# Clip to SBUF, exponential in place: attention with hashed buckets and a gated feed-forward

## The chip, the core and the metric

The kernel runs on one core of one Trainium2 chip. A core has TensorE (PE; its weight loads are listed apart as PEld), VectorE (DVE), ScalarE (ACT), GpSimd (POOL) and SyncE (SP, which here only issues DMAs), with a shared memory of 128 partitions (SBUF), and PSUM, into which TensorE writes. Each engine works through its own list of instructions in order and waits on semaphores for the others. The metric is the device time of one execution in microseconds. "Before" is the kernel without the change, "after" the kernel with it.

## The reference

Attention over buckets, for 4 batches, 8 heads, 768 positions and 64 columns a head, followed by a gated feed-forward:

```python
q_bits = (np.einsum('bhsd,dk->bhsk', q, proj) > 0).astype(np.int64)   # k_bits likewise
q_bucket = np.sum(q_bits * powers, axis=-1)                           # 6 bits
mask = q_bucket[:, :, :, None] == k_bucket[:, :, None, :]
scores = scale * np.matmul(q, k.transpose(0, 1, 3, 2))
scores = np.where(mask, scores, -1000000000.0)
scores = scores - np.max(scores, axis=-1, keepdims=True)
attn = np.exp(scores)
attn = attn / (np.sum(attn, axis=-1, keepdims=True) + 1e-09)
return np.matmul(attn, v).astype(np.float32)
```

A query whose bucket holds no key has the same score, -1e9, everywhere. Its softmax is flat, and its result is the mean of V. The heads' results, side by side (512 columns), then go through

```python
h = np.maximum(x @ w_in, 0.0)
u, v = (h[..., :d_ff // 2], h[..., d_ff // 2:])
v_n = (v - mu) / np.sqrt(var + 1e-06)
v_s = np.einsum('ts,bsd->btd', w_spatial, v_n) + b_spatial[None, :, None]
return ((u * v_s) @ w_out).astype(np.float32)
```

## The kernel before

**Numbers.** TensorE multiplies in f16. Each f32 operand is split into a high and a low f16 part. q and k are scaled by 32 for this. The hash bits of q and k are further rows of the same operands, so that the score matmuls themselves add a penalty, a multiple of 2^29 in the scaled scores, for each bit that differs. A score below -2^28 is thus one of an unmatched pair. The factor ISQ (1/8192) takes scaled scores back.

**Tiles.** There are 32 heads (n), each with six tiles (i) of 128 queries by 768 keys: global step g = 6n + i. Heads go in pairs p = n // 2, whose q, k and v are loaded together. Heads 1 to 7 (`KEYS`) have their keys on the partitions and go a way of their own (`row_max`, `scores_k`, `weighted_k`); they need the rows' maximum before the scores, but no transposition. The other 25 heads have queries on the partitions, 150 tiles in all. Such a tile passes these lines:

- L291, L292 (PE): four matmuls make the 128 x 768 scores in `sp`, a PSUM tile of two banks. There are two buffers of it (`PSB`).
- L293 (DVE): one pass over PSUM multiplies by -ISQ and takes the minimum along the row into `nb` (one column of a [128, 6] tile a head). The pass has to write its elements somewhere, and writes them as bf16 into the room of `ex` (`jk`), where nobody reads them.
- L294 (ACT): ex = exp(ISQ * scores + nb), from PSUM into SBUF, f32.
- L297 (ACT): the high f16 part of `ex`; L298: the low part, ex minus high, on DVE or, for one or two of six tiles, on POOL (`PL_POOL1`, `PL_POOL`).
- L300 (SP): a DMA transposes both halves, 128 x 1536 f16, into `pt`.
- L313 to L315 (PE): 18 matmuls with `pt` as weights add up the row of the result, and, through a column of ones beside V, the row's sum. They come five steps behind the scores (`LAG`).

**End of a head.** `normalize` (L317) divides by the sum. A row without a match has nb > ISQ * 2^28. For it the quotient is multiplied by zero (L329, DVE), and the mean of V times a flag (L323, L324, POOL) is added (L332, POOL). L337 and L338 split the sum `x` into f16 parts, and after the pair's second head L343 transposes them for the feed-forward. The mean of V comes from `mean_v`, once a pair: three additions on POOL (L224, L226, L227), a matmul with a matrix of ones (L229, f32, which TensorE runs as two), and a scaled copy (L231, ACT).

**Feed-forward.** The 28 units of batch b (`mlp_units`: v_unit, u_unit, s_unit, o_unit) are strewn among the tiles of batch b + 1, so many a step; the last batch's come at the end, with no attention beside them. The weights' conversion (`weights_gen`, L137 to L144) is strewn over steps 4 to 73 (`W_PTS`).

**What sets the order.** The program is traced step by step. `at(g, k)` sets a priority before each part, and a scheduler then fixes every engine's order at build time, by priority and by a planned timeline. Tiles of a tag share so many buffers (`bufs`): `ex` has EB = 3, `pp` PB = 4, `pt` PTB = 6; a new tile waits until the old one's last reader is done. SP issues nearly all DMAs: loads, the copies that build the operands (`build`, L192), transposes and results. ACT issues the hash rows' copies from head 8 on (L200, `BQ_S`).

## Time and profile before

| | |
|---|---|
| time, median of 3 runs | 726.72 us (724.35 to 730.93) |
| time of the profiled execution | 729.71 us |
| span of its instructions | 727.9 us |
| mean granted TensorE clock | 0.957 |
| busy: PE, PEld | 622.9 us (86%), 393.2 us (54%) |
| busy: DVE, ACT, POOL | 520.4 us (71%), 434.2 us (60%), 326.6 us (45%) |
| DMA | 120.96 MB, 290013 packets |

The profile's span runs from the first to the last instruction; the device time of the same execution is 1.8 us longer. A row of a group names the line, the engine, the operation, the tile written and those read (`out<-in`), the shape, and the count; then the busy time in us and the mean duration in ns, then the engine's idle time just before these instructions and what ended it. `ex<-sp` reads: writes `ex`, reads `sp`. A wait is put down to the one that was released last. "Chain" is the chain of work that ended last, followed backwards from the last instruction.

### The profile page before, as it was taken

What the parts mean: (1) busy time and instruction counts of PE and PEld (TensorE: products, weight loads), DVE (VectorE), ACT (ScalarE), POOL (GpSimd) and SP (SyncE); (2) the same over time, 40 slices, a digit from 0 to 9 for tenths busy, and PEclk for the clock granted to TensorE, in tenths of its full rate; (3) what the DMA queues carried; (4) which work ended last, traced back from release to release, by engine and by line L of the source; (5) the groups of instructions that cost most, each with busy time, mean ns of one, the idle gap of its engine ahead of it and who ended that gap; (6) DMA issues with size and microseconds to landing.
All of it is one profiled execution on the core that took longest, in us unless ns stands there. A gap on an engine that the chain in (4) does not pass through costs nothing. (4 is left out here: it accounts for less than half of the span.)

```text
span 727.9 us, 14930 instructions
## 1 busy us (share of the span) xinstructions
PE 622.9 (86%) x5759; PEld 393.2 (54%) x5759; DVE 520.4 (71%) x945; ACT 434.2 (60%) x668; POOL 326.6 (45%) x324
## 2 busy tenths in 40 slices
PE   1569897997987876998898899898989888999997
PEld 0237676875554543555555555565555555654553
DVE  4677894537899999768689887778699685845100
ACT  1345674356888677656667666667677677634221
POOL 5122542134479755446316672446146462441603
PEclk9969997999999988999999999999999999999999
DMA  9674745315999999997999999999999899860011
GB/s 238 151 140 146 170 132 105 94 47 131 233 247 210 212 198 203 218 210 161 223 213 186 193 202 183 228 197 206 228 227 169 167 168 210 147 157 10 1 44 44
DMA packets 290013, 120.96 MB, mean 166 GB/s; under 512 B 270741, under 2 KB 273813, under 8 KB 289941
## 3 DMA queue, kind: packets, MB, share of 16 engines
q1 hardware_dynamic: 287636, 119.11, 77.9%
q10 hardware_dynamic: 2304, 0.89, 0.5%
q8 instruction: 45, 0.74, 0.4%
q14 instruction: 28, 0.22, 0.1%
HBM read 28.33 MB, written 6.29 MB: 48 GB/s over the span
## 5 line engine op out<-in xcount | busy, mean ns | idle before, releaser
L294 ACT ACTIVATE ex<-sp,nb 128x768 f32<-128x768 f32 x150 | 134.6, 900 | 95.3 <-DVE ex L293 91.2
L293 DVE TENSOR_SCALAR_CACHE_REDUCE ex<-sp 128x768 bf16<-128x768 f32 x150 | 141.8, 949 | 43.2 <-PE sp L292 42.4
L298 DVE TENSOR_TENSOR pp<-ex,pp 128x768 f16<-128x768 f32 x116 | 125.9, 1091 | 20.7 <-ACT pp L297 20.5
L313 PE MATMUL pv<-vp,pt 128*128 128x65 f16 x900 | 105.5, 196 | 34.0 <-DMA pt<-pp 33.5
L291 PE MATMUL sp<-ab 128*128 128x384 f16 x300 | 102.2, 341 | 32.8 <-ACT ex L294 22.0
L297 ACT CAST pp<-ex 128x768 f16<-128x768 f32 x150 | 123.8, 830 | 10.6 <-ACT ex L294 2.5
L313 PEld LDWEIGHTS <-pt 128*128 128x128 f16 x900 | 85.4, 100 | 59.3 <-DMA pt<-pp 48.6
L298 POOL TENSOR_TENSOR pp<-ex,pp 128x768 f16<-128x768 f32 x34 | 58.2, 1711 | 123.9 <-ACT pp L297 101.1
L416 PE MATMUL sps<-ws,vn 128*128 128x384 f16 x576 | 103.9, 333 | 3.0 <-DVE sg L179 2.2
L314 PE MATMUL pv<-vp,pt 128*128 128x64 f16 x900 | 105.6, 195 | 0.0
L315 PE MATMUL pv<-vp,pt 128*128 128x65 f16 x900 | 105.3, 197 | 0.0
L292 PE MATMUL sp<-ab 127*128 127x384 f16 x300 | 102.4, 341 | 0.0
L314 PEld LDWEIGHTS <-pt 128*128 128x128 f16 x900 | 85.8, 99 | 10.7 <-issue 2.0
L315 PEld LDWEIGHTS <-pt 128*128 128x128 f16 x900 | 85.7, 99 | 3.7 <-issue 0.6
L416 PEld LDWEIGHTS <-vn 128*128 128x128 f16 x576 | 56.0, 100 | 40.7 <-issue 7.5
L431 PE MATMUL ops<-wo,g 128*128 128x512 f16 x288 | 70.0, 387 | 2.9 <-POOL wo L144 1.0
L401 PE MATMUL ups<-xt,wi 128*128 128x384 f16 x384 | 68.8, 331 | 0.0
L360 PE MATMUL vps<-wi,xt 128*128 128x512 f16 x288 | 67.1, 379 | 1.3 <-DMA xt<-xs 1.3
L332 POOL TENSOR_TENSOR x<-x,xf 128x384 f32<-128x384 f32 x32 | 36.8, 1151 | 69.7 <-DVE x L331 62.8
L274 PEld LDWEIGHTS pv<-vf,ex 128*128 128x128 f32 x504 | 65.6, 200 | 3.9 <-issue 1.1
L274 PE MATMUL pv<-vf,ex 128*128 128x65 f32 x504 | 64.5, 279 | 0.0
L421 POOL TENSOR_TENSOR sy<-sy,u 128x384 f32<-128x384 f32 x32 | 37.9, 1183 | 40.3 <-DVE sy L420 36.8
(87 smaller groups left out, 1006.1 us busy)
## 6 DMA issues: line engine op xcount, KB each, us to landing
qk<-kq SPq DMA_DIRECT2D x16, 768.0 KB
ab<-hl SPq DMA_DIRECT2D x31, 384.0 KB
ab<-hl SPq DMA_DIRECT2D x34, 192.0 KB
out<-o SPq DMA_DIRECT2D x24, 256.0 KB
v<-v SPq DMA_DIRECT2D x13, 384.0 KB
raw<-w_in SPq DMA_DIRECT2D x16, 256.0 KB
pt<-pp SPq DMA_TRANSPOSE x150
raw<-w_sp SPq DMA_DIRECT2D x12, 192.0 KB
```

What stands on the lines that cost most here:

```text
L274: nc.tensor.matmul(acc[:, qi, :], lhsT=ex[:, qi * P:(qi + 1) * P], rhs=vf[p % 2][:, 2 * i + e, :], start=(i == 0 and qi == 0), stop=(i == ...
L291: nc.tensor.matmul(ps[:, c], lhsT=t[:, 0, qs], rhs=t[:, 1, cs], start=True, stop=False)
L292: nc.tensor.matmul(ps[:, c], lhsT=t[0:P - 1, 3, qs], rhs=t[0:P - 1, 2, cs], start=False, stop=True)
L293: nc.vector.tensor_scalar(jk, ps, -ISQ, None, op0=ALU.mult, op1=ALU.min, accum_out=nb)
L294: st["ex", n, i] = nc.scalar.activation(ex, ps, AF.Exp, bias=nb, scale=ISQ).ins
L297: nc.scalar.copy(pp[:, 0], ex)
L298: (nc.gpsimd if i in (PL_POOL if n >= 2 * NH else PL_POOL1) else nc.vector).tensor_tensor(out=pp[:, 1], in0=ex, in1=pp[:, 0], op=ALU.subtract)
L313: nc.tensor.matmul(acc, lhsT=pt[:, c, :], rhs=vh, start=(i == 0 and c == 0), stop=False)
L314: nc.tensor.matmul(acc[:, 0:D], lhsT=pt[:, c, :], rhs=vl, start=False, stop=False)
L315: nc.tensor.matmul(acc, lhsT=pt[:, NT + c, :], rhs=vh, start=False, stop=(i == NT - 1 and c == NT - 1))
L416: nc.tensor.matmul(ps[:, :HS], lhsT=vn[gv][:, c, d * P:(d + 1) * P], rhs=ws[gw][:, c, hs], start=(k == 0), stop=(k == 3 * NT - 1))
L431: nc.tensor.matmul(ps, lhsT=gt[h][gg][:, c, j * P:(j + 1) * P], rhs=wo[gw][:, c, :], start=(k == 0), stop=(k == 3 * NF - 1))
```

## The change

For the 25 heads with queries on the partitions:

- The pass over PSUM now writes max(score, -2^28) as f32 into `ex` and takes the row's maximum into `mx`; the bf16 room is gone. A new operation on DVE makes nb = -ISQ * mx for the tile's column. The exponential reads `ex` in SBUF and writes it in place, so that the PSUM tile's last reader is the pass on DVE.
- A row without a match has -2^28 everywhere, so the exponential gives 1 in every place, and the quotient is the mean of V by itself. `normalize` loses the flag, the product with the mean, the zeroing and the addition in these heads.
- `mean_v` is left out for pairs without a key-oriented head (pairs 4 to 15). Its two scratch tiles, and the one in `normalize`, move to the tags `g0`, `g1` and `u`, which the feed-forward uses too; the tags `pf` and `vc` are gone.
- `ex` has four buffers in place of three, `mx` four in place of two.

In the heads 1 to 7 `normalize` keeps the flag, the product and the addition, and loses only the zeroing (L329), as their quotients there come out as zero.

```diff
@@ -218,11 +218,13 @@
         nc.vector.scalar_tensor_tensor(out=t[:, :, 0:D], in0=v32, scalar=SQ, in1=t[:, :, D:2 * D], op0=ALU.mult, op1=ALU.subtract)
 
     def mean_v(p):
+        if not has_keys(p):
+            return
         v32 = st["v32", p] if has_queries(p) else vf[p % 2][:, :, 0:D]
 
-        a = wk.tile([P, NT, D], F32, tag="pf", name=f"va{p}")
+        a = wk.tile([P, NT, D], F32, tag="g0", name=f"va{p}")
         nc.gpsimd.tensor_add(a, v32[:, 0:NT], v32[:, NT:2 * NT])
-        c = wk.tile([P, 2, D], F32, tag="vc", name=f"vc{p}")
+        c = wk.tile([P, 2, D], F32, tag="g1", name=f"vc{p}")
         nc.gpsimd.tensor_add(c, a[:, 0:2], a[:, 2:4])
         nc.gpsimd.tensor_add(c, c, a[:, 4:6])
         mp = ps_m.tile([P, 512], F32, tag=MT, name=f"mp{p}")
@@ -234,7 +236,7 @@
     def row_max(n, i):
         t = ab[n % NAB]
         if i == 0:
-            st["mx", n] = wk.tile([P, NT], F32, tag="mx", bufs=2, name=f"mx{n}")
+            st["mx", n] = wk.tile([P, NT], F32, tag="mx", bufs=4, name=f"mx{n}")
         ps = ps_sc.tile([P, 2, 512], F32, tag="sc", name=f"mp{n}_{i}")[:, :, :HS]
         for c in range(2):
             nc.tensor.matmul(ps[:, c], lhsT=t[0:P - 1, 3, i * P:(i + 1) * P],
@@ -281,17 +283,18 @@
         t = ab[n % NAB]
         if i == 0:
             st["nb", n] = wk.tile([P, NT], F32, tag="nb", bufs=3, name=f"nb{n}")
-        nb = st["nb", n][:, i:i + 1]
+            st["mx", n] = wk.tile([P, NT], F32, tag="mx", bufs=4, name=f"mx{n}")
+        mx, nb = st["mx", n][:, i:i + 1], st["nb", n][:, i:i + 1]
         ex = wk.tile([P, 2, HS], F32, tag="ex", bufs=EB, name=f"ex{n}_{i}")
-        jk = ex.rearrange("p c k -> p (c k)").bitcast(BF16)[:, 0:S].rearrange("p (c k) -> p c k", c=2)
         qs = slice(i * P, (i + 1) * P)
         ps = ps_sc.tile([P, 2, 512], F32, tag="sc", name=f"sp{n}_{i}")[:, :, :HS]
         for c in range(2):
             cs = slice(c * HS, (c + 1) * HS)
             nc.tensor.matmul(ps[:, c], lhsT=t[:, 0, qs], rhs=t[:, 1, cs], start=True, stop=False)
             nc.tensor.matmul(ps[:, c], lhsT=t[0:P - 1, 3, qs], rhs=t[0:P - 1, 2, cs], start=False, stop=True)
-        nc.vector.tensor_scalar(jk, ps, -ISQ, None, op0=ALU.mult, op1=ALU.min, accum_out=nb)
-        st["ex", n, i] = nc.scalar.activation(ex, ps, AF.Exp, bias=nb, scale=ISQ).ins
+        nc.vector.tensor_scalar(ex, ps, -float(2 ** 28), None, op0=ALU.max, op1=ALU.max, accum_out=mx)
+        nc.vector.tensor_scalar(nb, mx, -ISQ, None, op0=ALU.mult)
+        st["ex", n, i] = nc.scalar.activation(ex, ex, AF.Exp, bias=nb, scale=ISQ).ins
         at(NT * n + i + G_H, 50)
         pp = wk.tile([P, 2, 2, HS], F16, tag="pp", bufs=PB, name=f"pp{n}_{i}")
         nc.scalar.copy(pp[:, 0], ex)
@@ -317,19 +320,21 @@
     def normalize(n):
         p, e = divmod(n, 2)
         pv = st.pop(("pv", n))
-        nb = st.pop(("nb", n))
-        fl = wk.tile([P, NT], F32, tag="fl", bufs=2, name=f"fl{n}")
-        f = wk.tile([P, NT, D], F32, tag="pf", name=f"xf{n}")
-        nc.gpsimd.tensor_scalar(fl, nb, ISQ * 2 ** 28, None, op0=ALU.is_gt)
-        nc.gpsimd.tensor_mul(f, st["fm", p][:, e:e + 1, :].to_broadcast([P, NT, D]),
-                             fl.unsqueeze(2).to_broadcast([P, NT, D]))
         rv = wk.tile([P, NT], F32, tag="rv", bufs=2, name=f"rv{n}")
         nc.vector.tensor_scalar(rv, pv[:, :, D], 1e-9, 1.0 / SX if n in KEYS else SQ / SX, op0=ALU.add, op1=ALU.mult)
         nc.vector.reciprocal(rv, rv)
-        nc.vector.scalar_tensor_tensor(out=rv, in0=nb, scalar=ISQ * 2 ** 28, in1=rv, op0=ALU.is_le, op1=ALU.mult)
         x = wk.tile([P, NT, D], F32, tag="x", bufs=2, name=f"x{n}")
-        nc.vector.tensor_mul(x, pv[:, :, 0:D], rv.unsqueeze(2).to_broadcast([P, NT, D]))
-        nc.gpsimd.tensor_add(x, x, f)
+        if n in KEYS:
+            nb = st.pop(("nb", n))
+            fl = wk.tile([P, NT], F32, tag="fl", bufs=2, name=f"fl{n}")
+            f = wk.tile([P, NT, D], F32, tag="u", name=f"xf{n}")
+            nc.gpsimd.tensor_scalar(fl, nb, ISQ * 2 ** 28, None, op0=ALU.is_gt)
+            nc.gpsimd.tensor_mul(f, st["fm", p][:, e:e + 1, :].to_broadcast([P, NT, D]),
+                                 fl.unsqueeze(2).to_broadcast([P, NT, D]))
+            nc.vector.tensor_mul(x, pv[:, :, 0:D], rv.unsqueeze(2).to_broadcast([P, NT, D]))
+            nc.gpsimd.tensor_add(x, x, f)
+        else:
+            nc.vector.tensor_mul(x, pv[:, :, 0:D], rv.unsqueeze(2).to_broadcast([P, NT, D]))
         if e == 0:
             st["xs", p] = wk.tile([P, 2, NT, P], F16, tag="xs", bufs=2, name=f"xs{p}")
         xs = st["xs", p]
@@ -462,7 +467,7 @@
 
     RB = 3
     PB = 4
-    EB = 3
+    EB = 4
     PTB = 6
     XTB = 6
     LAG = 5
```

## The prediction

> **What bounds the kernel now.** The stretches of the span come first, because a share over the whole span mixes stages with different limits. The columns are busy time (and count) of TensorE, its weight loads, VectorE, ScalarE and GpSimd, then the granted clock, the share of the DMA engines and GB/s.
>
> ```profile
> 200.00:300.00 100.00, 77.05 (x821) 47.27 (x820) 97.43 (x163) 76.68 (x133) 69.18 (x59) 0.93 1.03 214
> 300.00:400.00 100.00, 89.74 (x939) 55.41 (x936) 77.50 (x145) 65.91 (x98) 43.94 (x41) 0.98 0.97 200
> 400.00:500.00 100.00, 89.62 (x941) 56.30 (x939) 80.56 (x137) 67.78 (x94) 50.64 (x45) 0.95 1.01 199
> 500.00:600.00 100.00, 90.20 (x950) 54.45 (x948) 82.86 (x154) 70.64 (x104) 49.48 (x44) 0.98 1.04 195
> 600.00:650.00 50.00, 47.43 (x537) 30.58 (x538) 33.76 (x64) 30.93 (x44) 20.80 (x20) 1.00 0.82 169
> 650.00:728.00 78.00, 72.59 (x393) 38.10 (x391) 14.72 (x36) 19.70 (x40) 22.98 (x23) 1.00 0.11 36
> ```
>
> There are three limits. From 200 to 300 us VectorE is busy 97.43 of 100 us: the conversion of the weights runs there beside the attention. From 300 to 650 us no engine is full: TensorE has 90 of 100, VectorE 77 to 83, and the DMA engines show shares of 0.97 to 1.04, so they are close to full as well. From 650 us on TensorE does the last batch's feed-forward nearly without a gap (72.59 of 78), and nothing of the change is in it. Before 170 us there are head 0 and the seven key-oriented heads, which the change leaves as they are but for head 0 (six tiles); I put that at 0.
>
> Next, what TensorE waits for between 180 and 650 us (total, times, longest).
>
> ```profile
> PE pv L313 <- DMA pt<-pp: 28.4, 28, 3.4
> PE sp L291 <- ACT ex L294: 19.5, 15, 2.6
> PE mp L229 <- POOL vc L227: 3.2, 5, 1.2
> ```
>
> The largest wait is for the transposed probabilities, which DMA brings. The second is for the exponential: score matmuls need one of two PSUM buffers, and the exponential of two tiles earlier holds it. The third is for GpSimd's sum of V. The change takes away the last two; where these waits lie decides what that is worth.
>
> Groups from 200 to 300 us, and from 300 to 650 us (busy, mean ns | idle before, its releaser):
>
> ```profile
> L293 DVE TENSOR_SCALAR_CACHE_REDUCE ex<-sp 128x768 bf16<-128x768 f32 x28 | 26.3, 946 | 1.7 <-PE sp L292 1.5
> L291 PE MATMUL sp<-ab 128*128 128x384 f16 x56 | 19.3, 344 | 13.5 <-ACT ex L294 13.4
> L329 DVE SCALAR_TENSOR_TENSOR rv<-nb,rv 128x6 f32<-128x6 f32 x4 | 0.8, 192 | 0.0
> L376 DVE TENSOR_SCALAR ve<-mv 128x3 f32<-128x3 f32 x2 | 1.8, 885 | 0.0
> ```
>
> ```profile
> L293 DVE TENSOR_SCALAR_CACHE_REDUCE ex<-sp 128x768 bf16<-128x768 f32 x104 | 98.4, 949 | 32.6 <-PE sp L292 32.0
> L291 PE MATMUL sp<-ab 128*128 128x384 f16 x206 | 68.2, 331 | 6.1 <-ACT ex L294 6.1
> L229 PE MATMUL mp<-vc,ones 128*128 128x128 f32 x16 | 3.9, 331 | 2.4 <-POOL vc L227 2.4
> L329 DVE SCALAR_TENSOR_TENSOR rv<-nb,rv 128x6 f32<-128x6 f32 x19 | 5.8, 306 | 0.5
> L376 DVE TENSOR_SCALAR ve<-mv 128x3 f32<-128x3 f32 x4 | 1.4, 354 | 0.0
> ```
>
> 13.4 us of the wait for the exponential lie in the stretch where VectorE is full, and only 6.1 us after it. In the first stretch the exponential is late because VectorE's clip pass before it is late, so freeing PSUM sooner gives VectorE no time back. Only the 6.1 us count.
>
> **The VectorE part.** The clip pass (L293) still reads 768 PSUM floats per partition and now writes f32 instead of bf16. Rows for its price:
>
> ```profile
> L293 DVE DVE_READ_ACCUMULATOR ex<-sp 128x1 f32 x150 | 12.1, 81 | 0.0
> L327 DVE TENSOR_SCALAR rv<-pv 128x6 f32<-128x6 f32 x32 | 5.1, 158 | 13.7 <-PE pv L315 7.3 <-PE pv L274 6.4
> L328 DVE RECIPROCAL rv<-rv 128x6 f32<-128x6 f32 x32 | 5.9, 186 | 0.6
> L331 DVE TENSOR_TENSOR x<-pv,rv 128x384 f32<-128x384 f32 x32 | 17.7, 552 | 0.6
> L298 DVE TENSOR_TENSOR pp<-ex,pp 128x768 f16<-128x768 f32 x116 | 125.9, 1091 | 20.7 <-ACT pp L297 20.5
> ```
>
> L331 reads PSUM and writes f32: 552 ns for 384 elements. L293 takes 397 ns more for 384 more, and L327, six elements out of PSUM, takes 158: the three lie on one line of some 155 ns and 1.03 ns an element, so an f32 write costs nothing extra: I take 0, with 0 and +142 ns (to L298's 1091, a full-size pass that reads SBUF operands) as bounds; the clip pass reads none. The accumulator read (81 ns) stays. New is one operation per tile, x150: [128,1] times a constant, behind the accumulator read. No such form is in the trace. The nearest rows are L327 (158 ns, a tensor_scalar too) and L328 (186 ns), which reads SBUF and follows its producer with almost no idle time; and on the other side L376, a tensor_scalar on three elements of SBUF: 354 ns on average from 300 to 650 us and 885 ns from 200 to 300 us. L329 (192 and 306 ns) also shows that small operations on SBUF operands are sometimes held. The bounds are 0.158 and 0.885 us. I take p = 0.17 us, between L327 and L328, because the new operand has one element.
>
> [...]
>
> VectorE also loses L329, in every head.
>
> **The GpSimd part.** The engines' sums over the span, and what goes away, with means:
>
> ```profile
> PE 622.9 (86%) x5759; PEld 393.2 (54%) x5759; DVE 520.4 (71%) x945; ACT 434.2 (60%) x668; POOL 326.6 (45%) x324
> L332 POOL TENSOR_TENSOR x<-x,xf 128x384 f32<-128x384 f32 x32 | 36.8, 1151 | 69.7 <-DVE x L331 62.8 <-DVE mv L369 6.9
> L324 POOL TENSOR_TENSOR xf<-fm,fl 128x384 f32<-128x384 f32 x32 | 33.4, 1043 | 2.0
> L323 POOL TENSOR_SCALAR fl<-nb 128x6 f32<-128x6 f32 x32 | 16.4, 513 | 50.7 <-DVE ex L293 35.2 <-DVE rv L329 10.8 <-DVE mv L369 4.2
> L224 POOL TENSOR_TENSOR va<-v 128x384 f32<-128x384 f32 x13 | 17.3, 1333 | 1.6 <-DMA v<-v 1.0
> L226 POOL TENSOR_TENSOR vc<-va 128x128 f32<-128x128 f32 x16 | 11.5, 716 | 2.1 <-PE mp L229 1.2
> L227 POOL TENSOR_TENSOR vc<-vc,va 128x128 f32<-128x128 f32 x16 | 9.9, 622 | 0.9
> ```
>
> Twenty-five heads lose L323, L324 and L332: 25 x (0.513 + 1.043 + 1.151) = 67.7 us. Twelve of sixteen pairs lose L224, L226 and L227: 12 x (1.333 + 0.716 + 0.622) = 32.1 us. That is 99.8 us of GpSimd's 326.6 (the first row), 31%. L298 on VectorE averages 1091 ns, where the line of above gives 155 + 1.03 x 768 = 946; so 145 x 116 = 16.8 us of it are holds. If they shrink as GpSimd's load does, 5.2 us come back over the span and 1.0 us in the 28 tiles from 200 to 300 us; other passes with SBUF operands are held as well, so I double that to 2.0 us (estimate). The first four pairs now share buffers g0, g1 and u with the first batch's feed-forward, which begins only after head 7; 0, or one wait of about 1 us (L324) without that distance. With these operations go two [128,128] f32 matmuls per pair (L229) and ScalarE's copy of the mean. The chain that ended last shows how such a mean stands in the way at 546 us (start, us, what):
>
> ```profile
> 546.87 1.00 POOL va L224
> ...
> 549.58 0.49 PE mp L229 x2
> 550.07 0.97 PE ups L401 x6
> ```
>
> TensorE's feed-forward (L401) waits in order behind the mean's matmul, which waits for three GpSimd operations.
>
> **The ScalarE part.** The exponential now reads SBUF:
>
> ```profile
> L264 ACT ACTIVATE ex<-sp 128x768 f32<-128x768 f32 x42 | 33.8, 805 | 29.4 <-PE sp L262 24.1 <-PE mp L240 3.0 <-DMA ab<-sg 2.1
> L217 ACT ACTIVATE vp<-v 128x768 f16<-128x768 f32 x13 | 11.0, 843 | 0.0
> L294 ACT ACTIVATE ex<-sp,nb 128x768 f32<-128x768 f32 x150 | 134.6, 900 | 95.3 <-DVE ex L293 91.2 <-DVE rv L329 1.3 <-DMA ab<-sg 1.3
> ```
>
> Without a bias the PSUM form takes 805 ns (L264) and the SBUF form 843 (L217), so I take 900 + 38 = 938 ns, with 900 and 938 + 38 as bounds. 150 x 0.038 = 5.7 us is hidden in ScalarE's idle time (65 to 71 of 100 us busy from 300 us on); without that cover it would be 5.7 us at most. The exponential starts p later than now, because it waits for the bias operation. Behind it on ScalarE is the tile's cast, and VectorE's or GpSimd's subtraction and the transpose on SP's queue wait for that. EB = 4 costs no instruction, and the clip pass waits for TensorE alone (32.0 of 32.6 us idle in L293's row), so the fourth buffer is put at 0.
>
> **The sum**, against the profiled execution (729.71 us, span 727.9):
>
> 200 to 300 us, VectorE bound: 28 tiles x 0.17 = +4.8, L329 -0.8, holds -2.0. That is +2.0.
>
> 300 to 650 us: L229 3.9 busy and 2.4 idle, -6.3. The wait for the exponential, -6.1: PSUM is now free after the clip pass, some 1 us sooner. GpSimd on the chain: here the shares of the chain from 500 to 650 us,
>
> ```profile
> by line: DMA pt<-pp 20.5%; issue 11.8%; PE ups L401 6.4%; DVE ex L293 6.0%; PE sps L416 4.9%; DVE pp L298 4.6%; POOL sy L421 4.1%; DMA ab<-hl 3.2%; POOL g L423 2.9%; POOL x L332 2.7%; PE vps L360 2.6%; PE sp L291 2.5%; POOL xf L324 2.5%; PE
> ```
>
> in which L332 and L324 hold 5.2% of 150 us, 7.8 us, or 18.2 us over 350. Another branch usually ends close behind, so I keep a third: -6.1. Against it, the clip pass is 6.0% of that chain, 9.0 us or 9.5 passes, 22 over 350 us; each becomes longer by p + 0.04 of the exponential: 22 x 0.21 = +4.6. Together -13.9. The transfers stay what they are and the DMA engines are near full until 600 us, so the wait for L313 takes some back; I let a third go: -9.3.
>
> End of the attention part:
>
> ```profile
> 650.54 1.00 POOL x L332
> ```
>
> The add L332 (1.00 us) stands alone between VectorE and ScalarE and goes: -1.0.
>
> +2.0 - 9.3 - 1.0 = -8.3, which makes 721.4 us of the profiled run. That run lies 3.0 us above the median of 726.72, so the forecast for a median is 726.7 - 8.3 = **718.4 us**. A measurement of this kernel tells about 1% (7.3 us) from no change.
>
> **The rivals.** *Larger gain:* nothing is taken back by DMA (-4.6), and all of the GpSimd chain is saved (-12.1 more): 726.7 - 8.3 - 16.7 = 701.7 us. For it speaks that both GpSimd parts and the PSUM wait are gone at once; against it the DMA shares near 1.0. Chance 0.12.
>
> *Hidden:* the transposes set the pace, so what TensorE no longer waits for at L291 and L229 it waits for at L313, with 28.4 us already the largest. Then only the +2.0 and the -1.0 are left: 727.7 us. The release of PSUM would then also fail to do what it is for: the wait moves to the clip pass. For it: DMA 0.97 to 1.04. Against it: from 600 to 650 us the share is 0.82, and TensorE is busy there. Chance 0.25.
>
> *Slower:* the new bias operation is held by GpSimd as L376 is, and VectorE's queue passes it to the clip pass and subtraction behind it. With 0.885 us for 28 tiles, 24.8 - 2.8 = +22.0 from 200 to 300 us; with 0.354 us in the rest, 22 x 0.184 = +4.0 more on the chain: +22.0 - 9.3 + 4.0 - 1.0 = +15.7, 742.4 us. With one p for both, the change is 50p - 16.8: even at p = 0.34 us and slower by 1% from p = 0.48 us. Against it: L328 is never held, and GpSimd has 31% less to do. Chance 0.21.
>
> **How the numbers follow.** The forecast's own case, 712 to 724 us, has 0.42, of which 0.06 lies within 1%. So faster by over 1%: 0.36 + 0.12 = 0.48; within 1%: 0.06 + 0.25 = 0.31; slower: 0.21. The range goes from 703, leaving out most of the larger gain, to 737, p = 0.54 us, leaving out the upper half of the slower case.
>
> **What would show it.** Right: a [128,1] row on VectorE x150 with a mean near 0.17 us; an f32 clip pass near 949 ns and an exponential near 938; L229 with 8 matmuls instead of 32; GpSimd near 227 us; no TensorE wait for the exponential. The forecast's discount is right if the wait for the transposed probabilities grows above 28.4 us while the others vanish. Wrong: a bias operation above 0.34 us, or VectorE at 97% beyond 300 us (slower); the same DMA share with an unchanged pace (hidden); or a TensorE above 94 of 100 us between 300 and 600 (larger gain).

## The result, and the profile after

After the change the kernel takes 739.85 us (median of 4 runs, 735.26 to 740.05), before it 725.66 us on the same chip (4 runs, 724.35 to 730.93). The ratio is 1.0154, with a 95% interval of 1.0112 to 1.0196: slower by 1.5%. (Ratios, here and below, leave out the runs that took over 1.5% more than the fastest of their kernel, and the profiled one of experiment 18, at 728.27 us, is just above that; medians and ranges are of all runs.) The forecast was 718.4 us. The profiled execution took 739.65 us, with a span of 737.8 us.

First the stretches of the kernel after; the columns are those of the prediction's table.

```profile
200.00:300.00 100.00, 80.63 (x856) 47.99 (x855) 92.59 (x198) 78.22 (x131) 48.74 (x40) 0.91 1.08 216
300.00:400.00 100.00, 87.16 (x869) 50.50 (x866) 69.62 (x157) 62.12 (x89) 24.95 (x19) 0.96 1.02 193
400.00:500.00 100.00, 89.76 (x975) 55.84 (x973) 76.89 (x164) 68.25 (x95) 27.14 (x20) 0.97 1.07 203
500.00:600.00 100.00, 88.62 (x941) 53.16 (x940) 85.97 (x184) 70.91 (x102) 30.37 (x23) 0.97 1.07 199
600.00:650.00 50.00, 45.82 (x517) 29.29 (x515) 35.51 (x81) 34.50 (x48) 10.17 (x8) 1.00 0.97 180
650.00:738.00 88.00, 81.97 (x499) 43.78 (x497) 17.76 (x41) 22.29 (x45) 25.80 (x26) 0.99 0.15 42
```

From 200 to 300 us VectorE is down from 97.4 to 92.6, and GpSimd has 19 to 24 us less in every hundred. TensorE has gained nothing from 300 to 650 us, and the DMA engines' share has gone up: 1.07 where it was 1.01 and 1.04, and 0.97 instead of 0.82 from 600 us on. After 650 us TensorE has 82 us of work left instead of 72.6.

What TensorE waits for in the kernel after, from 180 to 650 us:

```profile
PE pv L316 <- DMA pt<-pp: 51.6, 42, 4.1
PE sp L293 <- DVE ex L295: 7.5, 9, 2.3
PE vps L365 <- DMA xt<-xs: 1.7, 3, 0.7
```

The wait for the exponential is gone: PSUM is now handed back by the clip pass (L295), for 7.5 us instead of 19.5. The wait for the mean is not among the waits any more. But the wait for the transposed probabilities has gone from 28.4 to 51.6 us, more than the two gave.

The groups that the change touches, over the whole span of the kernel after:

```profile
PE 631.2 (86%) x5735; PEld 391.8 (53%) x5735; DVE 500.7 (68%) x1063; ACT 433.4 (59%) x656; POOL 223.3 (30%) x213
...
L295 DVE TENSOR_SCALAR_CACHE_REDUCE ex<-sp 128x768 f32<-128x768 f32 x150 | 141.7, 949 | 49.4 <-PE sp L294 48.3 <-POOL pp L301 0.5
L296 DVE TENSOR_SCALAR nb<-mx 128x1 f32<-128x1 f32 x150 | 21.3, 144 | 0.8
L297 ACT ACTIVATE ex<-ex,nb 128x768 f32<-128x768 f32 x150 | 138.0, 930 | 65.9 <-DVE nb L296 58.7 <-DVE ve L381 3.9 <-DMA ab<-sg 1.3
L301 DVE TENSOR_TENSOR pp<-ex,pp 128x768 f16<-128x768 f32 x116 | 121.7, 1053 | 31.5 <-ACT pp L300 30.9
L231 PE MATMUL mp<-vc,ones 128*128 128x128 f32 x8 | 3.2, 502 | 1.7 <-POOL vc L229 1.7
```

The clip pass writes f32 at 949 ns, as forecast. The bias operation L296 takes 144 ns and is never held (0.8 us of idle time ahead of 150 of them, and the longest took 155 ns). The exponential takes 930 ns. L301 on VectorE has lost 38 ns each. L231 has 8 matmuls, and GpSimd is busy for 223.3 us, forecast at 227. Every price of a single instruction was about right, and still the sum came out with the wrong sign.

### The profile page after: what moved, and what is told of

Same layout as the page of the kernel before. It is cut to its first block, busy times and chain, and to the rows that moved or that the text cites. A ratio compares the mean times of both kernels' runs of the same rounds, so it can differ in the third digit from the quotient of the medians.

```text
span 737.8 us, 14802 instructions
## 1 busy us (share of the span) xinstructions
PE 631.2 (86%) x5735; PEld 391.8 (53%) x5735; DVE 500.7 (68%) x1063; ACT 433.4 (59%) x656; POOL 223.3 (30%) x213
## 4 chain that ended last, share of the span: by engine, by line
PE 45%; DMA 27%; DVE 10%; issue 6%; ACT 5%; SPq 4%; POOL 2%; ACTq 1%; DVEq 0%; POOLq 0%
DMA pt<-pp 20%; PE ups L406 7%; PE pv L276 6%; PE vps L365 5%; PE ops L436 5%; PE sps L421 5%; DMA ab<-hl 4%; PE sp L293 3%; PE sp L294 2%; DVE pp L301 2%; PE pv L316 2%; DVE ex L295 2%; ACT pp L300 2%; PE pv L318 2%; PE pv L317 2%
## 5 line engine op out<-in xcount | busy, mean ns | idle before, releaser
L297 ACT ACTIVATE ex<-ex,nb 128x768 f32<-128x768 f32 x150 | 138.0, 930 | 65.9 <-DVE nb L296 58.7
L295 DVE TENSOR_SCALAR_CACHE_REDUCE ex<-sp 128x768 f32<-128x768 f32 x150 | 141.7, 949 | 49.4 <-PE sp L294 48.3
L316 PE MATMUL pv<-vp,pt 128*128 128x65 f16 x900 | 104.1, 197 | 56.7 <-DMA pt<-pp 56.4
L301 DVE TENSOR_TENSOR pp<-ex,pp 128x768 f16<-128x768 f32 x116 | 121.7, 1053 | 31.5 <-ACT pp L300 30.9
L300 ACT CAST pp<-ex 128x768 f16<-128x768 f32 x150 | 122.7, 825 | 23.7 <-DMA pt<-pp 20.5
L301 POOL TENSOR_TENSOR pp<-ex,pp 128x768 f16<-128x768 f32 x34 | 57.4, 1687 | 210.9 <-ACT pp L300 176.5
L317 PE MATMUL pv<-vp,pt 128*128 128x64 f16 x900 | 103.5, 196 | 0.0
L318 PE MATMUL pv<-vp,pt 128*128 128x65 f16 x900 | 103.4, 198 | 0.0
L421 PE MATMUL sps<-ws,vn 128*128 128x384 f16 x576 | 100.2, 326 | 1.6 <-DVE sy L425 1.3
L406 PE MATMUL ups<-xt,wi 128*128 128x384 f16 x384 | 74.1, 347 | 0.5 <-ACT vr L369 0.5
L365 PE MATMUL vps<-wi,xt 128*128 128x512 f16 x288 | 69.5, 389 | 1.7 <-DMA xt<-xs 1.7
L276 PE MATMUL pv<-vf,ex 128*128 128x65 f32 x504 | 66.7, 285 | 0.0
L266 ACT ACTIVATE ex<-sp 128x768 f32<-128x768 f32 x42 | 33.9, 806 | 38.4 <-PE sp L264 32.3
```

The source lines that it names most:

```text
L276: nc.tensor.matmul(acc[:, qi, :], lhsT=ex[:, qi * P:(qi + 1) * P], rhs=vf[p % 2][:, 2 * i + e, :], start=(i == 0 and qi == 0), stop=(i == ...
L295: nc.vector.tensor_scalar(ex, ps, -float(2 ** 28), None, op0=ALU.max, op1=ALU.max, accum_out=mx)
L297: st["ex", n, i] = nc.scalar.activation(ex, ex, AF.Exp, bias=nb, scale=ISQ).ins
L300: nc.scalar.copy(pp[:, 0], ex)
L301: (nc.gpsimd if i in (PL_POOL if n >= 2 * NH else PL_POOL1) else nc.vector).tensor_tensor(out=pp[:, 1], in0=ex, in1=pp[:, 0], op=ALU.subtract)
L316: nc.tensor.matmul(acc, lhsT=pt[:, c, :], rhs=vh, start=(i == 0 and c == 0), stop=False)
```

## The experiments

Each ratio is against runs of the kernel before on the same chip, next to the experiment's own. The numbers give the order in which they ran. What some of them seemed to say was overturned by experiments 13, 17 and 18; where that is so, it is said.

### Where the loss lies: experiments 1 to 4

The first theory blamed the planner: on VectorE 127 of the 150 bias operations stand behind one to seven other operations, so that the exponential starts 2.4 us behind the end of the clip pass on average, where it was under 0.5. Experiment 1 fixes the order of every engine as the kernel after has it, by an edge between neighbours; experiment 2 moves each bias operation directly behind its clip pass in that order.

```diff
+            for a, b in edges(traced):
+                tc.add_manual_dep(
+                    traced[b], a,
+                    mybir.DependencyInfo(mybir.DependencyClass.NoSync, mybir.DependencyReason.DATA),
+                    reason="pinned order")
...
+                row = [n for n, e in order if e == engine]
+                found += list(zip(row, row[1:]))
```

> The kernel after, with every engine's order of instructions fixed to the order that it has anyway; a control for the next run. All theories: as the kernel after, 735 to 741 us, 1.5% above before.

Measured: 744.08 us (735.9 to 745.9), ratio 1.0162 (1.0079 to 1.0245), the same as the kernel after. Fixing the order costs nothing that shows.

```diff
+                row = [m for n in row if n not in follows for m in ((n, pairs[n]) if n in pairs else (n,))]
```

> The kernel after with the same fixed order on all engines, but on VectorE each bias operation stands directly behind its clip pass; in the kernel after 127 of 150 have one or more other operations between. Theory 1 (the place of the bias operation in VectorE's order delays the exponential, and with it the transposed probabilities): the time from the end of the clip pass to the bias operation falls from 1.2 us to under 0.2, TensorE's wait for the transposed probabilities falls well under 56.4 us, and the time to 722 to 732 us. Theory 2 (one more dependent operation in the chain costs this wherever it stands): 736 us or more, the wait about the same.

Measured: 747.18 us (744.05 to 751.89), ratio 1.0248 (1.0161 to 1.0334). No gain, rather a loss, and the first theory falls: the bias operation starts 0.03 us behind its clip pass, where it was 1.2 us in the kernel after, but the exponential comes only 0.5 us earlier, and TensorE's wait for the transposed probabilities over the span stays at 57.0 us (56.4 in the kernel after).

Experiment 3 has the in-place part alone (f32 clip, bias operation, exponential in SBUF, `mx` with four buffers; old `normalize`, `mean_v` and EB), experiment 4 the end of the head alone (new `normalize`, no mean for pairs 4 to 15, scores as before, so that rows without a match in heads 0 and 8 to 31 do not get the mean).

```diff
-            st["mx", n] = wk.tile([P, NT], F32, tag="mx", bufs=2, name=f"mx{n}")
+            st["mx", n] = wk.tile([P, NT], F32, tag="mx", bufs=4, name=f"mx{n}")
...
-        nc.vector.tensor_scalar(jk, ps, -ISQ, None, op0=ALU.mult, op1=ALU.min, accum_out=nb)
-        st["ex", n, i] = nc.scalar.activation(ex, ps, AF.Exp, bias=nb, scale=ISQ).ins
+        nc.vector.tensor_scalar(ex, ps, -float(2 ** 28), None, op0=ALU.max, op1=ALU.max, accum_out=mx)
+        nc.vector.tensor_scalar(nb, mx, -ISQ, None, op0=ALU.mult)
+        st["ex", n, i] = nc.scalar.activation(ex, ex, AF.Exp, bias=nb, scale=ISQ).ins
```

> The clip into SBUF, the bias operation and the exponential in place, with the mean of V, the end of a head and three ex buffers as before. Theory 1: as slow as after or slower, 738 to 750 us, since the loss is in this part and GpSimd's relief is missing. Theory 3 (the loss comes with the new end of a head): as before, 720 to 732 us.

Measured: 739.82 us (738.77 to 742.56), ratio 1.0131 (1.0073 to 1.0189).

```diff
     def mean_v(p):
+        if not has_keys(p):
+            return
...
-        nc.vector.scalar_tensor_tensor(out=rv, in0=nb, scalar=ISQ * 2 ** 28, in1=rv, op0=ALU.is_le, op1=ALU.mult)
...
+        else:
+            nc.vector.tensor_mul(x, pv[:, :, 0:D], rv.unsqueeze(2).to_broadcast([P, NT, D]))
```

> The kernel before with the new end of a head and without the means of pairs 4 to 15: the sum of the mean of V for rows without a match is left out. Theory 1: this part is a gain by itself, 712 to 723 us. Theory 3: slower than before, 733 us or more.

Measured: 726.75 us (722.17 to 730.56), ratio 0.9943 (0.9907 to 0.9979). The loss lies in the part with the scores, to which the four buffers of `mx` belong; 100 us less of GpSimd are worth 0.6%.

### Order or operations: experiments 5 and 6

The next two theories were the planner's order (2) and the operations themselves (3). Experiment 5 takes the order of every engine from the kernel before, with the bias operation behind its clip pass; experiment 6 is the mirror for TensorE.

```diff
+    first, names, order = built(ORDER_OF, lambda names: [])
+    place = {n: k for k, n in enumerate(common(names))}
...
+                if e == engine and n in place:
+                    m = mine[place[n]]
+                    row += [m, pairs[m]] if m in pairs else [m]
```

> The operations of the third experiment (clip to SBUF, bias operation right behind it, exponential in place; old end of a head) with every engine's instructions in the order that they have in the kernel before. Theory 2 (the loss is the planner's other order: it sees the score buffer freed sooner and places scores, the gated layers and the transposes otherwise): the loss goes, 725 to 731 us, ratio 0.995 to 1.005. Theory 3 (the loss is the operations themselves: the chain from the scores to the transposed probabilities is 2 to 3 us longer per tile, and TensorE reaches the product five tiles later whatever the order): 736 to 743 us, ratio 1.010 to 1.020, wait for the transposed probabilities 50 us or more.

Measured: 745.97 us (742.99 to 749.37), ratio 1.0243 (1.0179 to 1.0307). That seemed to prove theory 3; experiment 13 takes it back.

```diff
+PINNED = (ET.PE,)
+ORDER_OF, OPS_OF = True, False
```

> The mirror: the operations of the kernel before (bf16 clip, exponential from PSUM, no bias operation), but TensorE's instructions in the order of the third experiment; the other engines' order is planned afresh for that. Theory 2 (order): 735 to 743 us, ratio 1.008 to 1.020, wait for the transposed probabilities above 45 us. Theory 3 (operations): 723 to 731 us, ratio 0.99 to 1.005.

Measured: 756.66 us (752.8 to 761.08), ratio 1.039 (1.0318 to 1.0462), slower than either theory had it. TensorE's longest wait there, over the span:

```profile
PE sp L295 <- ACT ex L305: 38.3, 32, 3.3
```

The wait for the exponential is back and longer than it was (22.0 us in the kernel before). Probably TensorE's order of the in-place kernel counts on PSUM that comes free sooner than the old operations give it; that was not tried apart. It tells the two theories apart no further.

### With half of the transposes: experiments 7 and 8

In both, every engine keeps the order that the kernel has with whole transposes.

```diff
-        st["tr"] = nc.sync.dma_start_transpose(out=pt, in_=pp.rearrange("p g c k -> p (g c k)")).ins
+            st["tr"] = nc.sync.dma_start_transpose(out=pt[:, 0:NT], in_=pp[:, 0].rearrange("p c k -> p (c k)")).ins
...
-            nc.tensor.matmul(acc, lhsT=pt[:, NT + c, :], rhs=vh, start=False, stop=(i == NT - 1 and c == NT - 1))
+            nc.tensor.matmul(acc, lhsT=pt[:, c if HALF[-1] else NT + c, :], rhs=vh, start=False, stop=(i == NT - 1 and c == NT - 1))
```

> The kernel before in its own order, with only the high half of each tile's probabilities transposed (half the elements of the 150 transposes; the low half's products take the high half again, so the low half is left out of the result). Theory D (from 200 to 650 us the DMA engines set the pace, and whatever is taken off TensorE's other waits comes back as the wait for transposed probabilities): 40 us or more faster, ratio 0.95 or less, and the wait for transposed probabilities under 10 us. Rival (TensorE and VectorE set the pace there): under 20 us faster, ratio above 0.973.

Measured: 701.07 us (700.83 to 704.21), ratio 0.9635 (0.9579 to 0.969).

> The changed kernel in its own order with the same half of the transposes left out. Theory D: with the transposes out of the way the removed waits count, and it is 5 us or more faster than the kernel before with half of the transposes. Theory 2 or 3 without D: it stays 8 to 14 us slower than that, as with whole transposes.

Measured: 693.47 us (690.58 to 698.13), ratio 0.9524 (0.9446 to 0.9602). TensorE's waits over the whole span, the first block from experiment 7, the second from experiment 8:

```profile
PE sp L295 <- ACT ex L298: 21.8, 16, 2.9
PE mp L233 <- POOL vc L231: 13.3, 11, 2.2
...
PE pv L320 <- DMA pt<-pp: 4.7, 6, 2.5
```

```profile
PE sp L297 <- DVE ex L299: 20.3, 18, 3.3
...
PE pv L323 <- DMA pt<-pp: 7.7, 8, 2.1
```

With the wait for the transposed probabilities down to 5 and 8 us the order of the two kernels turns round: the changed one is 7.6 us ahead (693.47 against 701.07). Experiment 7 itself gained 27 us, between what theory D and its rival had said. So the change has a gain, and with whole transposes it is lost.

### The bias operation and the place of the exponential, apart: experiments 9 to 11

Both halves of the in-place part in the order of the kernel before, and the second also planned afresh. Without a bias operation the pass multiplies by -ISQ and takes the minimum, as it did before, but keeps the elements.

```diff
+            a = nc.vector.tensor_scalar(jk, ps, -ISQ, None, op0=ALU.mult, op1=ALU.min, accum_out=mx)
+            b = nc.vector.tensor_scalar(nb, mx, 1.0, None, op0=ALU.mult)
```

> The kernel before in its own order on every engine, with one thing added: the clip pass accumulates into a separate tile and a one-element operation behind it on VectorE makes the bias (150 times, times 1.0); the exponential reads PSUM as before. Theory 3a (the price is the extra link between the clip pass and the exponential: 154 ns of it and 43 ns before it in the fifth experiment, 150 x 0.197 = 29.6 us of VectorE of which the fifth experiment lost 18): 739 to 748 us, ratio 1.014 to 1.026. Theory 3b (the price is that the exponential works in SBUF on f32 scores: 33 ns longer each, more traffic at the DMA's memory): 724 to 731 us, ratio 0.995 to 1.005.

Measured: 749.64 us (746.76 to 752.67), ratio 1.028 (1.0223 to 1.0337).

```diff
+            nc.vector.tensor_scalar(ex, ps, -ISQ, None, op0=ALU.mult, op1=ALU.min, accum_out=nb)
+            st["ex", n, i] = nc.scalar.activation(ex, ex, AF.Exp, bias=nb, scale=-1.0).ins
```

> The other half, again in the order of the kernel before: VectorE writes the scores times -1/8192 as f32 to SBUF with their minimum, and the exponential runs there in place with scale -1 and that minimum as bias, so no bias operation is needed (the clip is not there; rows without a match are given the mean by the old end of a head). Theory 3a: 723 to 731 us, ratio 0.994 to 1.005. Theory 3b: 738 to 748 us, ratio 1.013 to 1.026.

Measured: 738.61 us (736.83 to 739.99), ratio 1.0127 (1.0076 to 1.0177).

```diff
-        nc.vector.tensor_scalar(ex, ps, -float(2 ** 28), None, op0=ALU.max, op1=ALU.max, accum_out=mx)
-        nc.vector.tensor_scalar(nb, mx, -ISQ, None, op0=ALU.mult)
-        st["ex", n, i] = nc.scalar.activation(ex, ex, AF.Exp, bias=nb, scale=ISQ).ins
+        nc.vector.tensor_scalar(ex, ps, -ISQ, None, op0=ALU.mult, op1=ALU.min, accum_out=nb)
+        st["ex", n, i] = nc.scalar.activation(ex, ex, AF.Exp, bias=nb, scale=-1.0).ins
```

> The operations of the tenth experiment planned afresh (the third experiment without its bias operation; the whole computation is done). Theory 3a: the planner's gain from the score buffers freed sooner comes without the price, 714 to 726 us, ratio 0.98 to 0.997, faster than the kernel before. Theory 3b: 735 to 745 us, ratio 1.01 to 1.02.

Measured: 731.19 us (728.18 to 735.23), ratio 1.0029 (1.0002 to 1.0057). Neither theory 3a nor 3b fits: the ninth goes the way of 3a, a little beyond its range, the tenth goes against it, and the eleventh is between them. The two halves of experiment 5 add up to 4.1%, and together they cost 2.4%. Something that all of them share had not been named.

### A tile more of distance: experiments 12 and 16

```diff
-    LAG = 5
+    LAG = 6
```

> The changed kernel with the product of a tile six instead of five tiles behind its scores (one number). Theory L (the wait for transposed probabilities is the latency of a tile's chain, 17 to 18 us, against the five tiles of 3.2 us that TensorE runs ahead): the wait falls from 56 to under 30 us and the time to 731 us or less, ratio 1.005 or less. Theory D (the DMA engines' rate sets it): wait 45 us or more, 735 to 745 us, ratio 1.01 to 1.02.

Measured: 734.19 us (730.91 to 737.54), ratio 1.0078 (1.0039 to 1.0118). (With this one edit the last tile of a pair is multiplied by the next pair's V, whose split comes first; the work is the same. In experiment 16 the split of V and the mean come a step later.)

```diff
-                if i == 5 and r + 1 < NP:
-                    split_v(r + 1)
-                    mean_v(r + 1)
...
+                if i == 0 and r + 1 < NP:
+                    split_v(r + 1)
+                    mean_v(r + 1)
...
-    LAG = 5
+    LAG = 6
```

> The kernel before with the product six tiles behind the scores; the values of a pair are split one tile later so that the last tile of the pair before still finds its own (the whole computation is done). Theory L (latency of the chain against the tiles that TensorE runs ahead; the twelfth experiment gave 5 to 6 us of 10): 718 to 725 us, ratio 0.985 to 0.996. Theory D (rate of the DMA engines alone): 725 to 732 us, ratio 0.997 to 1.005.

Measured: 723.91 us (718.65 to 729.09), ratio 0.9964 (0.993 to 0.9998). The distance is worth 0.4% in the kernel before and some 0.8% in the kernel after; but in experiment 12 the wait for the transposed probabilities, over the span, is still

```profile
PE pv L316 <- DMA pt<-pp: 47.1, 36, 4.3
```

so latency is a part of it and not the whole.

### The control that turned it: experiment 13, and 14

Experiment 13 is the control of the fifth, ninth and tenth: the operations of the kernel before, in their own order, fixed the same way. The lines are against the fifth.

```diff
-ORDER_OF, OPS_OF = False, True
+ORDER_OF, OPS_OF = False, False
```

> The kernel before, its own operations in its own order, with that order fixed on every engine in the way of the fifth, ninth and tenth experiments. If fixing the order costs nothing: 724 to 731 us, ratio 0.995 to 1.005, and those three show their operations' cost. If the fixing itself costs (8 us or more, ratio 1.011 or more), that much has to be taken off the three.

Measured: 740.77 us (739.34 to 742.9), ratio 1.0204 (1.0159 to 1.0248), for the same instructions in the same order on every engine. Over the span TensorE waits in the kernel before (first block) and in experiment 13 (second):

```profile
PE pv L313 <- DMA pt<-pp: 33.5, 32, 3.4
PE sp L291 <- ACT ex L294: 22.0, 16, 2.6
```

```profile
PE pv L324 <- DMA pt<-pp: 47.1, 36, 3.5
PE sp L295 <- ACT ex L305: 21.2, 14, 2.9
```

The wait for the exponential is as it was, the one for the transposed probabilities is not. So 2% of the fifth, ninth and tenth experiments was neither their operations nor the order. What is left of them against the thirteenth is 1.0243 / 1.0204 = +0.4%, +0.7% and -0.8%.

Experiment 14 has the edits of the ninth and the seventh together:

```diff
+            b = nc.vector.tensor_scalar(nb, mx, 1.0, None, op0=ALU.mult)
...
+            st["tr"] = nc.sync.dma_start_transpose(out=pt[:, 0:NT], in_=pp[:, 0].rearrange("p c k -> p (c k)")).ins
```

> The ninth experiment (old order, bias operation added, exponential from PSUM) with half of each tile's transpose left out as in the seventh (701.1 us there; the low half is left out of the result). Theory C (closed loop: the 0.2 us count only because TensorE then waits for the transposed probabilities, which with half transposes it does for 5 us only): 699 to 707 us. Theory 3a alone (150 x 0.2 us of VectorE lie on the chain whatever the transposes do): 715 to 724 us.

Measured: 714.57 us (711.77 to 717.36), ratio 0.984 (0.9793 to 0.9887): 13.5 us above experiment 7. At the time this spoke for theory 3a; but it has the thirteenth's hidden difference in it, and how the 13.5 us divide was not tried. The traces say that little of it is a wait for the transfers: over the span TensorE waits for the transposed probabilities about as long as in experiment 7 (5.0 against 4.7 us), and longer for the exponential (29.9 against 21.8).

The hidden difference is where the tiles lie. Experiment 13 was built on the third, with four buffers of `mx` that are first asked for in `scores`, ahead of `ex`. A buffer of it takes 32 bytes of a partition, so `ex`, `pp` and `pt` begin 128 bytes later. From the built programs, the first byte of `pp` and `pt` in a partition, and from the packets in the traces, the 261162 packets of 256 bytes that a kernel with whole transposes has (experiments 7, 8 and 14 have 145962):

| kernel | pp, pt | modulo 512 | mean, ns | 30 ns or longer | ratio |
|---|---|---|---|---|---|
| before | 133632, 145920 | 0 | 22.2 | 1.7% | 1 |
| 4: end of head | 133632, 145920 | 0 | 23.1 | 2.7% | 0.9943 |
| 16: before, six tiles | 133632, 145920 | 0 | 22.1 | 1.8% | 0.9964 |
| after | 136832, 149120 | 128 | 23.7 | 6.6% | 1.0154 |
| 3: in place only | 133760, 146048 | 128 | 23.9 | 7.8% | 1.0131 |
| 11: in place, no bias op | 133760, 146048 | 128 | 23.8 | 7.6% | 1.0029 |
| 13: old order, old operations | 133760, 146048 | 128 | 24.0 | 8.2% | 1.0204 |

Experiments 1, 2, 5, 6, 8, 9, 10, 12 and 14 are at 128 too, with 5.9 to 8.3% of long packets, experiment 7 at 0 with 2.2%. The kernel after asks for `mx` at the same spot.

### The place alone: experiments 17 and 18

Two kernels in which only the place moves; the order of every engine is, instruction for instruction, that of the kernel before and of the kernel after. In experiment 17 everything from `ex` on lies 128 bytes further on, in experiment 18 everything from `ex` on 384 bytes.

```diff
-            st["nb", n] = wk.tile([P, NT], F32, tag="nb", bufs=3, name=f"nb{n}")
+            st["nb", n] = wk.tile([P, NT], F32, tag="nb", bufs=7, name=f"nb{n}")
```

> The kernel before, same operations, same order on every engine, with the small tile of biases given seven buffers instead of three: 128 bytes more per partition ahead of the exponential, so that the tiles read and written by the big transposes start at 128 instead of 0 modulo 512 bytes, as they do in the changed kernel. Theory P (place in SBUF: every kernel so far with these tiles at 0 modulo 512 was fast for its kind, every one at 128 slow, the thirteenth experiment by 14 us with the same operations and order): 736 to 744 us, ratio 1.013 to 1.023, and the transposes' 256-byte packets 24 ns instead of 22. Rival (fixing the order cost the 14 us of the thirteenth; the place is nothing): 724 to 731 us, ratio 0.995 to 1.005.

Measured: 741.59 us (737.58 to 748.24), ratio 1.0223 (1.0164 to 1.0283); 23.8 ns a packet, 8.0% of them 30 ns or longer. That is the loss of experiment 13 (1.0204) without a fixed order, so fixing it was free. Measured by experiment 17 rather than by the kernel before, experiments 9, 3 and 11 stand at +0.6%, -0.9% and -1.9%, and the kernel after at -0.7%.

```diff
-            st["mx", n] = wk.tile([P, NT], F32, tag="mx", bufs=4, name=f"mx{n}")
+            st["mx", n] = wk.tile([P, NT], F32, tag="mx", bufs=16, name=f"mx{n}")
```

> The changed kernel, same operations, same order on every engine, with the small tile of maxima given sixteen buffers instead of four: the tiles of the big transposes start at 0 modulo 512 bytes again. Theory P: 14 to 20 us less than the changed kernel, 718 to 727 us, ratio 0.983 to 0.999. Rival (the bias operation and the order are the loss): 736 to 744 us, ratio 1.012 to 1.02.

Measured: 725.52 us (717.35 to 730.47), ratio 0.9957 (0.9918 to 0.9996); 22.7 ns, 2.6%. The place is worth 2.2% in the one kernel and, by 0.9957 / 1.0154, 1.9% in the other, 14 to 16 us each; the intervals of each pair are far apart (0.9996 at most against 1.0112 at least in the second). Both went as theory P had it. Next the DMA queue of the four kernels (packets, MB, time of the packets as a share of 16 engines' span): before, experiment 17, after, experiment 18.

```profile
q1 hardware_dynamic: 287636, 119.11, 77.9%
```

```profile
q1 hardware_dynamic: 287636, 119.11, 79.8%
```

```profile
q1 hardware_dynamic: 287636, 119.11, 80.0%
```

```profile
q1 hardware_dynamic: 287636, 119.11, 79.7%
```

The packets and the bytes are the same to the last one. Times the span that is 567 us in the kernel before, 594 us with nothing but the place changed; 590 us in the kernel after and 579 us moved back. Worked out so for all kernels with whole transposes, it is 567 to 584 us at 0 and 589 to 595 us at 128. In every kernel most of the 256-byte packets take 18 ns (94% of them in the kernel before, 85% in the kernel after), and in those with whole transposes some 760 to 1000 take over 400 ns, at either place. What moves with the place is the number between 30 and 100 ns: 3169 in the kernel before and 19398 in experiment 17, 15633 in the kernel after and 5421 in experiment 18.

TensorE's waits from 180 to 650 us, in experiment 17 and then in 18:

```profile
PE pv L313 <- DMA pt<-pp: 38.9, 33, 3.2
PE sp L291 <- ACT ex L294: 19.5, 13, 2.9
PE mp L229 <- POOL vc L227: 2.7, 3, 1.2
```

```profile
PE pv L316 <- DMA pt<-pp: 38.1, 35, 3.1
PE sp L293 <- DVE ex L295: 8.0, 8, 2.4
```

In experiment 17 the exponential and the mean keep TensorE waiting as they did before (19.5 and 2.7 us), and the wait for the transposed probabilities alone has grown, by 10.5 us. In experiment 18 it is 13.5 us below that of the kernel after.

The transposes of the heads' results (L343 in the kernel before, `xt<-xs`) tell more of the place. The last of them comes when the large ones are done, so that its 1536 packets of 256 bytes can be read apart (the places are from the built programs again):

| kernel, or number of experiment | `xs`, `xt` modulo 512 | packets of 30 ns or longer |
|---|---|---|
| before, 7, 16 | 256, 256 | none |
| after, 1, 2, 8, 12, 15 | 256, 320 | none |
| 4 | 192, 256 | 12% |
| 18 | 128, 192 | 12% |
| 3, 5, 6, 9, 10, 11, 13, 14 | 320, 320 | 12% |
| 17 | 384, 384 | 12% |

For this transpose it is thus the source tile that counts and not the target, and a source at 256 modulo 512 had no packet of 30 ns or longer. For the large ones only 0 and 128 were tried, with source and target together.

### A version that beats both: experiment 15

The bias operation is needed because the maximum has to be multiplied by -ISQ. If the scores come out of TensorE negated and in the exponent's unit, the minimum is the bias.

```diff
-HQ = 16384.0
-HK = 32768.0
+SK = 8.0 ** -0.5
+HQ = -16384.0
+HK = 4.0
...
-        nc.scalar.activation(hl[:, 1:3], qk, AF.Copy, scale=SQ)
+        nc.scalar.activation(hl[:, 1], qk[:, 0], AF.Copy, scale=-SK)
+        nc.scalar.activation(hl[:, 2], qk[:, 1], AF.Copy, scale=SK)
...
-        nc.vector.tensor_scalar(ex, ps, -float(2 ** 28), None, op0=ALU.max, op1=ALU.max, accum_out=mx)
-        nc.vector.tensor_scalar(nb, mx, -ISQ, None, op0=ALU.mult)
-        st["ex", n, i] = nc.scalar.activation(ex, ex, AF.Exp, bias=nb, scale=ISQ).ins
+        nc.vector.tensor_scalar(ex, ps, float(2 ** 15), None, op0=ALU.min, op1=ALU.min, accum_out=nb)
+        st["ex", n, i] = nc.scalar.activation(ex, ex, AF.Exp, bias=nb, scale=-1.0).ins
```

In heads 1 to 7 `row_max` then takes the minimum and `scores_k` has an exponential with scale -1.

> The changed kernel without its bias operation, the whole computation kept: queries and keys are scaled by 8 to the power -1/2 and the keys negated, so PSUM holds minus the score; VectorE writes min(that, 32768) to SBUF with the minimum, which is the bias as it stands; the exponential runs in place with scale -1. Unmatched rows still give the mean by themselves. If the bias operation is the price: 1.0 to 1.4% below the changed kernel, 722 to 731 us, ratio 0.992 to 1.003. If it is the in-place exponential or the planner's order: 735 us or more.

Measured: 716.31 us (711.67 to 718.01), ratio 0.986 (0.9816 to 0.9904), below the expected 722 to 731, because two things went at once: `mx` is not asked for in `scores` any more, so the tiles are back at 0 modulo 512 (2.0% long packets). Against experiment 18, which has the bias operation and the same place, 0.986 / 0.9957 leaves 1.0% for the bias operation (with whatever the second scaling copy costs, and with `xs`, which lies at 256 here and at 128 in experiment 18). TensorE's waits in experiment 15, from 180 to 650 us:

```profile
PE pv L316 <- DMA pt<-pp: 27.7, 24, 3.6
PE sp L294 <- DVE ex L296: 14.3, 10, 3.8
```

The wait for the transposed probabilities is down to 27.7 us, under that of the kernel before, with the wait for PSUM at 14.3.

## Why the prediction was wrong

**The step that failed** is the sentence "The transfers stay what they are". Packets and bytes did; where they read and write did not. The prediction priced the buffers by their instructions (the fourth buffer of `ex` "is put at 0") and passed over the four buffers of `mx`, which stand ahead of `ex`, `pp` and `pt` and push them 128 bytes on. That cost 14 us (1.9%, experiment 18 against the kernel after), in the one resource that the prediction had itself found to be close to full (DMA shares of 0.97 to 1.04 from 200 to 600 us), and it is more than the whole forecast gain of 8.3. It was in no rival.

**The sum without it** is -0.43% by experiment 18, of 727.9 us -3.1 us (interval -6.0 to -0.3), where -8.3 was forecast: right in sign, too large. In the profiled executions (spans of 727.9 us in the kernel before and 726.2 in experiment 18) the difference divides so: up to the clip pass of the 46th of the 150 tiles, at 298 us in both, +0.3 us (forecast +2.0); from there to the last tile's clip pass -6.2 (forecast -9.3); from there to the last product +3.5 (forecast -1.0); behind that +0.7. The term that is furthest off here is the end of the attention part. The add L332 went, but the last tile's exponential starts 2.4 us after its clip pass does, where it was 1.0, and its first product 10.9 us after, where it was 7.4. This rests on one execution of each kernel, and experiment 18's was 2.8 us above the median.

The third that the DMA takes back from 300 to 650 us was about right. Of TensorE's waits there, the one for the exponential (6.1 us) and the one for the mean (2.4) are gone in experiment 18, and the wait for the transposed probabilities grows by 2.6; before, then experiment 18:

```profile
PE pv L313 <- DMA pt<-pp: 22.1, 20, 3.4
```

```profile
PE pv L316 <- DMA pt<-pp: 24.7, 21, 3.1
```

From 180 to 300 us the waits for PSUM and for the mean lose 6.2 us, and the wait for the transposed probabilities gains 7.0 (6.3 to 13.3): nothing is left, which fits the prediction's "Only the 6.1 us count".

At the same place the two parts of the change do not add up. At 0 the new end of a head alone has 0.9943 (experiment 4) and the whole change 0.9957; at 128, measured by experiment 17, the part with the scores alone has -0.9% (experiment 3) and the whole change -0.7%, with intervals of some half a per cent each. Experiments 7 and 8 show the other end: with half of the transposes the change is worth 7.6 us even in its bad place.

**The bias operation** was well priced. In the sum it stood with 4.8 us from 200 to 300 us and 22 x 0.17 = 3.7 us after that, together 8.5. Measured it is 1.0% planned afresh, by experiments 18 and 15 at 0 and by 3 and 11 at 128 modulo 512, some 7 us; 0.7 to 1.1% in the old order (9 against 13, 5 against 10). Nor was it held. In the kernel before, L376 had a GpSimd operation beside it four times in eight; it then took 0.32 to 0.89 us and ended within 0.03 us of the end of a GpSimd operation, and the other four times it took 0.15 to 0.17 us. Of the 150 bias operations in the kernel after, 40 had a GpSimd operation beside them: they took 142 ns on average and 154 at most, the other 110 took 145 and 155.

**The slower rival** named a time near the measured one, 742.4 us, for a cause that did not happen: it needed a bias operation of 0.48 us, and it took 0.144. (Its line 50p - 16.8 leaves out the third that the sum takes back; with it the change is 43p - 15.5, even at 0.36 us and slower by 1% from 0.53.) **The hidden rival** was nearest to what the change does once the place is taken out; it had 727.7 us, and experiment 18 lies between it and the forecast. **Larger gain** had 701.7 us, and no kernel with whole transposes came near it: the best, experiment 15, takes 716.3 us and needs the bias operation gone for it.

**The end of the head** was put at GpSimd off the chain (-6.1 before a third went), the mean's matmuls (-6.3) and the last add (-1.0). Alone it gave 0.6%, 4 us (experiment 4). There the wait for the exponential fell from 22.0 to 7.3 us over the span although the exponential still read PSUM, but the wait for the transposed probabilities grew from 33.5 us to

```profile
PE pv L315 <- DMA pt<-pp: 49.7, 42, 4.2
```

**What stays open**: whether for the large transposes too it is the place of the source, `pp`, that counts, and whether 256 modulo 512 bytes would do for it, as `ex`, `pp` and `pt` moved together and only to 0 and 128 (the packets that became longer are of the transposes' size); why some of the packets are hit and not all, 12% of those of the last `xt<-xs`; and a part of the 12 us of packets between the kernel before (567) and experiment 18 (579). Some 6 of them are packets of 30 to 100 ns, more in experiment 18, whose `xs` lies at 128; the rest is mostly in packets of over 400 ns. That the places of all later tiles moved as well was not taken apart.

## What to carry to other kernels

Before a change to a kernel like this one, with DMA shares near 1, is judged, compare the first bytes of the tiles that the large transposes read and write, modulo 512: here 128 in place of 0 cost 14 to 16 us. A small tile or a buffer more ahead of them moves them all, here by 128 bytes for four buffers of `mx`. A control that has the same operations in the same order and only the means of the experiment is worth its run before the experiments that lean on it: here it came thirteenth and overturned most of what had been read from the twelve before it. And with the DMA engines at shares of 0.97 to 1.09 (from 200 to 600 us, before and in experiment 18), a part of the wait taken off TensorE came back as the wait for the transfer: at the same place all of it from 180 to 300 us and a third from 300 to 650.

## What the runs showed of the hardware that was not expected

- 128 bytes of place, nothing else, cost 14 us in 728: transposes of 128 x 1536 f16 from and to tiles at 128 modulo 512 bytes had 6 to 8% of their 256-byte packets at 30 ns or longer, at 0 modulo 512 only 1.7 to 2.7%.
- A transpose of the same kind by itself, 1536 packets of 256 bytes, had no packet of 30 ns or longer when its source tile lay at 256 modulo 512 bytes, whether its target lay at 256 or at 320, and 12% of them when the source lay at 128, 192, 320 or 384.
- The operation that reads the accumulator's result on one element took 154 ns directly behind its clip pass (23 times in the kernel after) and 143 ns where others stood between (127 times); the row of experiment 2, where all stand directly behind, shows the first:

```profile
L299 DVE TENSOR_SCALAR nb<-mx 128x1 f32<-128x1 f32 x150 | 23.0, 154 | 5.2
```

- Runs of one kernel on one chip spread over 10 us (experiment 16: 718.65 to 729.09), so that a single profiled execution does not show differences of 1%.
